# Loading k, v and q of the next batch but one at the end of slot 3, with q split first

## The chip, the cores and the metric

One NeuronCore of a Trainium2 chip runs the whole program; inputs and output lie in device memory. The metric is the device time of one execution in microseconds (us). The engines are PE (TensorE, matrix products; PEld is its weight load), DVE (VectorE), ACT (ScalarE), POOL (GpSimd) and SP (SyncE, which only issues DMAs here). Each works through its own instructions strictly in the order in which the program lists them; an instruction that waits holds up everything behind it on its engine.

## The reference

Three layers, one after the other. Shapes: 8 batches, 8 heads, 576 tokens, head width 64, 32 memory slots.

```
a    = softmax of phi over the tokens                        # per batch, head, slot
k_m  = a^T k ;  v_m = a^T v                                  # 32 x 64 per head
attn = softmax(q k_m^T / 8) ;  x = attn v_m                  # 4608 tokens x 512
g    = s * relu(x w_in)^2 + b ;  x2 = g w_out                # 512 -> 2048 -> 512
h    = x2 w_in2 ;  e = h * softmax(h) ;  out = layernorm(e) * g_ln @ w_out2
```

## The kernel before

Products that need more than half precision are made of three products of halves: an operand is split into a high and a low float16 part (`split_hi` on ACT, line 277; `split_lo` on DVE, line 280), after scaling by a power of two.

The order of the work is written out by hand. A long list of steps, `FIRST`, does batch 0, the decoding of the weights and part of batch 1. Then a loop over n = 1 to 7 does the feed-forward layer of batch n in two halves j (288 tokens each): `gemm1` (line 934) makes eight products of 12 matmuls into one of three PSUM buffers `hp`, and ACT takes each out with `relu` (line 945) and a square (line 970); DVE makes the two halves of the result (lines 920 and 977). Then four `gemm2` (line 994) follow, one for each d, each taken out by ACT (line 1011) and stored by SP (`gemm2_put`, line 1022). Before each `gemm2`, one of eight slots prepares the attention of batch n + 1:

- slots 0 and 1: the memory products `kv_mm`; the k and v of the batch are four pieces in three buffers, and piece 3 is loaded in slot 0. At the end of slot 1 the kernel before issues phi (line 295) and k, v pieces 0 to 2 (line 321) of batch n + 2. `q_abs` and `q_scale` find the scale of q.
- slot 2: `mem_scale`, `mem_hi`, `mem_lo` split the memory keys and values, and `mem_tr` (line 726) transposes them by DMA; then `q_split` of q pieces 0 and 1. A `q_split` is `q_hi` on ACT, `q_lo` on DVE, a transposing DMA `q_tr` (line 760) and, in the kernel before, the load of the same piece of batch n + 2 (line 331).
- slot 3: `q_split` of pieces 2 and 3, `phi_max`. The split goes to a work buffer with room for two pieces, so `q_hi` of piece 2 waits until `q_tr` of piece 0 has landed, and piece 3 waits for piece 1.
- slots 4 to 6: scores, softmax, and the transposing DMA `scores_T`; slots 4 to 7: `vw`, the memory values times w_in.

`gemm1` of the second half comes right after slot 3. Its first `relu` stands on ACT behind `q_hi` of pieces 2 and 3.

During n = 1 also w_in is split, in four pieces (`w_in_split`, before slots 0 to 5 in turn): ACT and DVE write a piece into `wt_s`, and SP moves it by four DMAs (`w_in_move`, line 606); the next piece waits for that move. In some slots `early` decodes a part of the third layer's weights: ACT's first step (line 228) waits for the DMA of line 1188, which the slot before issued on SP. In n = 5 such a decode stands in slot 3, in the other n not.

All DMAs of the loop are issued by SP, in program order.

Of the kernel before, what the change touches and what calls it, by code (L numbers as in the profile page):

```python
# [57 lines left out]
def tile_mem_attention__moe_relu2__solu_ln(  # L58
# [15 lines left out]
    nc = tc.nc  # L74
    NB, H, S, D = q.shape
# [4 lines left out]
    C = 6  # L80
# [4 lines left out]
    KD = DM // 128  # L85
# [57 lines left out]
    q_s = q_p.tile([128, 3, C, 2, D], FP32, name="q_s")  # L143
# [3 lines left out]
    def flat(t):  # L147
        n = len(t.shape)
        if n == 2:
            return t  # L150
        ax = " ".join("abcdef"[:n - 1])
        return t.rearrange(f"p {ax} -> p ({ax})")
# [120 lines left out]
    def absmax(out_, in_):  # L273
        nc.vector.tensor_reduce(out=out_, in_=in_, op=ALU.max, axis=AX, apply_absolute_value=True)  # L274

    def split_hi(hi, lo, src, sc):
        nc.scalar.activation(out=hi, in_=src, func=ACTF.Copy, scale=sc[:, 0:1])  # L277

    def split_lo(hi, lo, src, sc):
        nc.vector.scalar_tensor_tensor(  # L280
            out=lo, in0=src, scalar=sc[:, 0:1], in1=hi, op0=ALU.mult, op1=ALU.subtract
        )
# [6 lines left out]
    phi_t, kv_t, q_t = {}, {}, {}  # L289

    def load_phi(n):
        if n >= NB:
            return
        t = phi_p.tile([P, H, C, M], FP32, tag="phi", name="phi_sb")
        nc.sync.dma_start(
            out=t.rearrange("p h c m -> p h (c m)"), in_=phi[n].rearrange("h (p c) m -> p h (c m)", c=C)
        )
        phi_t[n] = t
# [8 lines left out]
    def q_place(n, i):  # L307
        if n and (n == 1 or i == 3):
            t = flat(wt_s)[:, i * C * 2 * D:]
        elif i == 3:  # L310
            t = flat(w_out_t[0]).bitcast(FP32)
        else:
            return q_s[:, i]
        return t[:, 0:C * 2 * D].rearrange("p (c h d) -> p c h d", c=C, h=2)

    def load_kv(n, i):
        if n >= NB:
            return
        t = kv_place(n, i)[0:P]
        for a, src in enumerate((k, v)):  # L320
            nc.sync.dma_start(
                out=t[:, a], in_=src[n, 2 * i:2 * i + 2].rearrange("h (p c) d -> p h (c d)", c=C)
            )
        kv_t[n, i] = t

    def load_q(n, i):
        if n >= NB:
            return
        t = q_place(n, i)[0:P]
        for a in range(2):  # L330
            nc.sync.dma_start(out=t[:, :, a, :], in_=q[n, 2 * i + a].rearrange("(p c) d -> p c d", c=C))  # L331
        q_t[n, i] = t


    es_t, km_t, qT_t, aT_t = {}, {}, {}, {}
# [4 lines left out]
    def phi_max(n):  # L340
        if n >= NB:
            return
        pm = e_p.tile([P, H, 1, M], FP32, tag="es", name="pm", bufs=1)
        phi_tree(n, pm[:, :, 0, :], ALU.max)
        if n < 2:
            px_t[n] = pm
            return
        px = e_p.tile([P, H, 1, M], FP32, tag="px", name="px", bufs=1)
        px_t[n] = pm, px

    def phi_tree(n, out_, op):
        ph = phi_t[n]
        t = e_p.tile([P, H, 2, M], FP32, tag="e", name="t")
        nc.vector.tensor_tensor(out=t, in0=ph[:, :, 0:2, :], in1=ph[:, :, 2:4, :], op=op)
        nc.vector.tensor_tensor(out=t, in0=t, in1=ph[:, :, 4:6, :], op=op)
        nc.vector.tensor_tensor(out=out_, in0=t[:, :, 0, :], in1=t[:, :, 1, :], op=op)
# [64 lines left out]
    def kv_mem(n, g):  # L421
        kv_mm(n, g)
        kv_sum(n, g)
        kv_out(n, g)
# [41 lines left out]
    def kv_out(n, g):  # L466
        kp = kp_t.pop((n, g))
        if g == 0:
            km_t[n] = e_p.tile([128, 2, 2 * D], FP32, tag="km", name="km", bufs=1)
        rs = st.tile([128, 1], FP32, tag="rs", name="rs")  # L470
        nc.vector.tensor_scalar(out=rs, in0=kp[:, 1, 0:1], scalar1=1e-9, scalar2=None, op0=ALU.add)
        nc.vector.reciprocal(out=rs, in_=rs)
        nc.vector.tensor_scalar(
            out=km_t[n][:, g], in0=kp[:, 0, 0:2 * D], scalar1=rs[:, 0:1], scalar2=None, op0=ALU.mult
        )
        if g == 0:
            if n > 1:
                load_kv(n, 3)
        else:
            phi_t.pop(n)  # L480
            es_t.pop(n, None)
            if n > 1:
                load_next_kv(n + 1)

    def load_next_kv(n):
        load_phi(n)
        for i in range(3):
            load_kv(n, i)

# [157 lines left out]
    def mem_all(n):  # L647
        al = st.tile([128, 2], FP32, tag="alb", name="al")
        nc.gpsimd.partition_all_reduce(out_ap=al, in_ap=bnd_t[n], channels=128, reduce_op=RED.max)
        bnd_t[n] = al  # L650
# [22 lines left out]
    def mem_scale(n):  # L673
        inv = st.tile([128, 2], FP32, tag="invb", name="inv")
        sc = pow2_scale(bnd_t.pop(n), inv, "scb", 2)
        sc_t[n] = c15
        cs = st.tile([128, KD], FP32, tag="cs", name="cs", bufs=2)
        t = st.tile([128, 1], FP32, tag="csa", name="csa", bufs=2)
        u = st.tile([128, 1], FP32, tag="csu", name="csu")
        nc.vector.tensor_tensor(out=u, in0=inv[:, 1:2], in1=iwin, op=ALU.mult)  # L680
        nc.vector.tensor_tensor(out=t, in0=s22, in1=u, op=ALU.mult)
        nc.vector.tensor_tensor(out=t, in0=t, in1=u, op=ALU.mult)
        csc_t[n] = cs, t
        msc_t[n] = sc
        es = st.tile([P, 1], FP32, tag="esc", name="esc", bufs=2)
        nc.vector.scalar_tensor_tensor(
            out=es, in0=inv[0:P, 0:1], scalar=scale, in1=qsc_t[n][1], op0=ALU.mult, op1=ALU.mult
        )
        esc_t[n] = es
# [3 lines left out]
    def work(i):  # L693
        if ("w", i) not in gt:
            gt["w", i] = raw_p.tile([128, 4096], FP16, tag="raw", name="work")
        return gt["w", i]
# [16 lines left out]
    def mem_hi(n):  # L713
        for ops in mem_ops(n):
            split_hi(*ops)

    def mem_lo(n):
        for ops in mem_ops(n):
            split_lo(*ops)
# [9 lines left out]
    qsc_t, esc_t = {}, {}  # L729

    def q_abs(n, i):
        if n not in qsc_t:
            qsc_t[n] = st.tile([P, KD], FP32, tag="qmx", name="qmx")
        absmax(qsc_t[n][:, i:i + 1], q_t[n, i].rearrange("p c h d -> p (c h d)"))

    def q_scale(n):
        mx = st.tile([P, 1], FP32, tag="qm", name="qm")
# [4 lines left out]
    def q_ops(n, i):  # L742
        u = slice((i % 2) * 1536, (i % 2 + 1) * 1536)
        qs = (work(0) if n > 1 else flat(kv_s[:, 2]).bitcast(FP16))[0:P, u]
        return qs, qs.rearrange("p (c h a d) -> p c h a d", c=C, h=2, a=2)

    def q_hi(n, i):
        qs = q_ops(n, i)[1]
        split_hi(qs[:, :, :, 0, :], None, q_t[n, i], qsc_t[n][0])

    def q_lo(n, i):
        qs = q_ops(n, i)[1]
        split_lo(qs[:, :, :, 0, :], qs[:, :, :, 1, :], q_t.pop((n, i)), qsc_t[n][0])

    def q_tr(n, i):
        if n > 1:
            qT = flat(qt_s).bitcast(FP16).rearrange("p (i x t) -> p i x t", i=KD, t=P)[:, i]
        else:
            qT = work(i // 2)[:, 0:24 * P].rearrange("p (i x t) -> p i x t", i=2, t=P)[:, i % 2]
        nc.sync.dma_start_transpose(out=qT, in_=q_ops(n, i)[0])  # L760
        qT_t[n, i] = qT.rearrange("p (c h) t -> p c h t", c=C)

    def q_split(n, i):
        q_hi(n, i)
        q_lo(n, i)
        q_tr(n, i)
        load_q(n + 1, i)

    def scores_mm2(n, cp):
        sp = ps_h.tile([128, 2, 512], FP32, tag="h", name="sp")  # L770
# [101 lines left out]
    def slot(n, i):  # L872
        if n >= NB:
            return
        if i == 0:
            kv_mem(n, 0)
            q_abs(n, 0)
            q_abs(n, 1)
        elif i == 1:
            kv_mem(n, 1)  # L880
            mem_bound(n)
            mem_all(n)
            q_abs(n, 2)
            q_abs(n, 3)
            q_scale(n)
        elif i == 2:
            mem_scale(n)
            mem_hi(n)
            mem_lo(n)
            mem_tr(n)  # L890
            q_split(n, 0)
            q_split(n, 1)
        elif i == 3:
            q_split(n, 2)
            q_split(n, 3)
            phi_max(n + 1)
            phi_all(n + 1)
        elif i == 4:
            scores_vw(n, 0)
        elif i == 5:  # L900
            scores_vw(n, 1)
        elif i == 6:
            scores_vw(n, 2)
        else:
            vw(n, 3)
            phi_sub(n + 1, nc.gpsimd)
            phi_exp(n + 1)
# [568 lines left out]
    with tc.manual_schedule():  # L1476
# [11 lines left out]
        for step in FIRST.split():  # L1488
            name, _, at = step.partition(".")
# [91 lines left out]
```

## Time and profile before

| | us |
|---|---|
| three runs, median (lowest, highest) | 1152.99 (1150.55, 1153.09) |
| the profiled execution, its time | 1154.11 |
| its span, first to last instruction | 1152.3 |
| PE busy | 1066.1 |
| DVE busy | 804.9 |
| ACT busy | 515.8 |
| POOL busy | 243.5 |

The `FIRST` list ends near 196 us, the loop over n runs to about 783 us, with about 81 us for one n, and then the third layer fills the rest, with PE busy nearly without a break. In the rows below, "us, us, engine line" of a timeline are the start, the duration, the engine and the line of the code; what stands in brackets is the engine's idle time before the instruction and who ended it.

### The profile page before, as it was taken

The numbers are of one execution on the slowest core, as the hardware profiler recorded it, in microseconds if no ns is written. First come the engines' busy times: TensorE is split into PE (matmuls) and PEld (weight loads), VectorE is DVE, ScalarE is ACT, GpSimd is POOL, SyncE is SP. The second block draws the span as 40 slices with busy tenths as digits, with TensorE's granted clock in tenths as the row PEclk, the third lists the DMA queues.
The fourth block names the chain that finished last, engine by engine and source line by source line (L and its number), as shares of the span: only waits on it lengthen the run. The fifth ranks groups of instructions, "written<-read, shape, count | busy, mean of one in ns | idle before, by whom it ended". The sixth has DMA issues, their size and how long they took to land.

```text
span 1152.3 us, 20462 instructions
## 1 busy us (share of the span) xinstructions
PE 1066.1 (93%) x8208; PEld 694.4 (60%) x8208; DVE 804.9 (70%) x1551; ACT 515.8 (45%) x745; POOL 243.5 (21%) x181
## 2 busy tenths in 40 slices
PE   0777699979999999999989999999999999999997
PEld 0644466756777777777767777765444444444443
DVE  5989968757776866876686786637666666666662
ACT  4365355444464455455355456623333333333332
POOL 2345721002103003012012010002222222222220
PEclk9778899989999999999999999999999999999999
DMA  9958143785392572662842414113445444455335
GB/s 289 264 142 206 39 81 88 174 151 125 100 189 65 131 145 70 161 115 65 197 104 67 122 32 164 58 44 84 102 104 110 101 107 93 103 110 101 81 67 101
DMA packets 246368, 134.00 MB, mean 116 GB/s; under 512 B 177152, under 2 KB 234496, under 8 KB 246272
## 3 DMA queue, kind: packets, MB, share of 16 engines
q1 hardware_dynamic: 246176, 132.68, 50.1%
q8 instruction: 64, 1.05, 0.4%
q14 instruction: 32, 0.26, 0.1%
q0 software_dynamic: 96, 0.01, 0.0%
HBM read 71.83 MB, written 23.07 MB: 82 GB/s over the span
## 4 chain that ended last, share of the span: by engine, by line
PE 66%; DVE 5%; DMA 3%; ACT 2%; SPq 2%; issue 1%; POOL 1%; POOLq 0%; ACTq 0%; DVEq 0%
PE y L994 21%; PE hp L1327 16%; PE y L1409 15%; PE hp L934 10%; PE wp L626 1%; PE kp L432 1%; DMA work<-in_moe_w_out_dram 1%; DMA qt_s<-work 1%; DVE g L977 1%; PE sp L773 1%; SPq L760 1%; DMA kv_s<-in_v_dram 1%; SPq L331 0%; DVE wt_s L280 0%; DMA w_in_t<-wt_s 0%
## 5 line engine op out<-in xcount | busy, mean ns | idle before, releaser
L994 PE MATMUL y<-g,w_out 128*128 128x288 f16 (+1 forms) x2880 | 366.2, 288 | 7.4 <-DVE first L180 6.9
L994 PEld LDWEIGHTS <-w_out 128*128 128x128 f16 x3072 | 297.9, 98 | 100.6 <-issue 20.4
L934 PE MATMUL hp<-aT,vwt 128*128 128x288 f16 x1536 | 199.4, 291 | 17.4 <-ACT r L945 14.1
L1409 PE MATMUL y<-w_t,lt 128*128 128x512 f16 x864 | 192.0, 379 | 1.8 <-DMA lt<-nat 1.8
L1327 PE MATMUL hp<-w_t,xs 128*128 128x512 f16 x864 | 192.2, 379 | 0.0
L934 PEld LDWEIGHTS <-vwt 128*128 128x128 f16 x1536 | 151.8, 99 | 62.0 <-issue 20.5
L1409 PEld LDWEIGHTS <-lt 128*128 128x128 f16 x864 | 84.4, 98 | 103.8 <-DMA lt<-nat 2.3
L1327 PEld LDWEIGHTS <-xs 128*128 128x128 f16 x864 | 84.5, 98 | 101.5
L1371 POOL TENSOR_TENSOR rstd<-ve,nhalf 128x1 f32<-128x1 f32 x36 | 52.7, 1463 | 336.1 <-DVE mv L1369 336.1
L1341 DVE TENSOR_REDUCE hmx<-hp 128x1 f32<-128x1024 f32 x36 | 44.1, 1224 | 86.7 <-PE hp L1327 86.7
L277 ACT ACTIVATE xs<-xt,xsc 128x512 f16<-128x512 f32 x36 | 26.0, 721 | 151.3 <-PE hp L1327 129.9
L977 DVE TENSOR_TENSOR g<-r,g 128x576 f16<-128x576 f32 x115 | 89.8, 780 | 5.5 <-POOL r L972 1.6
L970 ACT ACTIVATE r<-r 128x576 f32<-128x576 f32 x118 | 80.6, 683 | 22.4 <-DVE g L977 18.2
L1011 ACT ACTIVATE x<-y,bcol,cs 128x288 f32<-128x288 f32 x64 | 37.4, 584 | 113.6 <-PE y L994 84.3
L945 ACT ACTIVATE r<-hp 128x576 f32<-128x576 f32 x120 | 76.7, 640 | 10.7 <-PE hp L934 6.7
L1348 ACT ACTIVATE e<-hp,nm,xiv 128x1024 f32<-128x1024 f32 x36 | 43.3, 1202 | 46.2 <-DVE nm L1343 46.2
L274 DVE TENSOR_REDUCE xmx<-x 128x1 f32<-128x288 f32 x64 | 28.6, 447 | 46.0 <-ACT x L1011 46.0
L920 DVE CAST g<-r 128x576 f16<-128x576 f32 x112 | 51.3, 458 | 10.9 <-ACT r L970 10.8
L849 POOL TENSOR_TENSOR e<-e,ssm 96x512 f32<-96x512 f32 x21 | 21.9, 1045 | 171.1 <-DVE ssm L844 169.0
L1417 ACT ACTIVATE o<-y,io 128x512 f32<-128x512 f32 x36 | 24.7, 687 | 51.7 <-issue 43.2
L1385 DVE TENSOR_TENSOR nat<-so,nat 128x1024 f16<-128x1024 f32 x36 | 43.8, 1216 | 5.4 <-ACT nat L1380 5.4
L1364 DVE BATCH_NORM_STATS2 bs<-so 128x6 f32<-128x512 f32 x72 | 46.3, 685 | 1.3
(239 smaller groups left out, 1213.0 us busy)
## 6 DMA issues: line engine op xcount, KB each, us to landing
x_d<-x SPq DMA_DIRECT2D x64, 144.0 KB, 2.8
xt<-x_d SPq DMA_DIRECT2D x36, 256.0 KB, 3.2
kv_s<-in_k_dram SPq DMA_DIRECT2D x31, 288.0 KB, 7.3
kv_s<-in_v_dram SPq DMA_DIRECT2D x31, 288.0 KB, 7.5
q_s<-in_q_dram SPq DMA_DIRECT2D x42, 144.0 KB, 4.0
phi_sb<-in_phi_dram SPq DMA_DIRECT2D x8, 576.0 KB, 6.2
out_dram<-o SPq DMA_DIRECT2D x24, 192.0 KB, 2.4
raw<-in_moe_w_out_dram SPq DMA_DIRECT2D x4, 1024.0 KB, 7.8
```

The costliest lines, as they stand in the source:

```text
L920: nc.vector.tensor_copy(out=g_of(n, j, 0)[:, 2 * fp:2 * fp + 2, 0:BLK], in_=gt["r2", j, fp])
L934: nc.tensor.matmul(out=hp[:, u, 0:BLK], lhsT=vt[:, pw, R, f * 128:(f + 1) * 128], rhs=aT[:, CJ * j:CJ * (j + 1), pa, R, :], start=(x == 0) ...
L945: nc.scalar.activation(out=r, in_=gt.pop(("h", j, fp))[:, :, 0:BLK], func=ACTF.Relu, scale=scale)
L970: nc.scalar.activation(out=r2, in_=r, func=ACTF.Square)
L977: (nc.vector if eng == "D" else nc.gpsimd).tensor_tensor(out=g_of(n, j, 1)[:, fs, 0:BLK], in0=gt.pop(("r2", j, fp)), in1=g_of(n, j, 0)[:, ...
L994: nc.tensor.matmul(out=y[:, 0:w], lhsT=w_out_t[d][:, pw, f, :], rhs=g_of(n, j, pg)[:, f, 0:w], start=(x == 0), stop=(x == len(steps) - 1),)
L1327: nc.tensor.matmul(out=hp[:, a, :], lhsT=xs[:, px, kk, :], rhs=wt[:, pw, kk, a * 512:(a + 1) * 512], start=(kk == 0 and px == 0 and pw == ...
L1341: nc.vector.tensor_reduce(out=mx, in_=hv, op=ALU.max, axis=AX)
L1364: nc.vector.bn_stats(out=bs[:, a, :], in_=so[:, a * 512:(a + 1) * 512])
L1371: nc.gpsimd.tensor_tensor(out=rstd, in0=ve, in1=nhalf, op=ALU.pow)
L1385: nc.vector.tensor_tensor(out=nat[:, 1, :], in0=so, in1=nat[:, 0, :], op=ALU.subtract)
L1409: nc.tensor.matmul(out=y[:, 0:DM], lhsT=lt[:, pl, f, :], rhs=wt[:, pw, f, :], start=(x == 0), stop=(x == len(steps) - 1),)
```

## The change

Three things. q_s keeps the two heads of a piece one after the other instead of interleaved, for all batches but the first, so that one partition of one head is one run of 6 x 64 numbers in memory; the transposed q is indexed to match. The load of q moves out of `q_split`, and the load of k, v pieces 0 to 2 out of slot 1; both stand in one function `load_next` that slot 3 calls after its `q_split`s: eight q DMAs, then six for k and v. phi keeps its place. And slot 2 does `q_split` 0 and 1 ahead of the memory's scale, split and transpose.

```
@@ q_place
-            return q_s[:, i]
-        return t[:, 0:C * 2 * D].rearrange("p (c h d) -> p c h d", c=C, h=2)
+            t = flat(q_s[:, i])
+        t = t[:, 0:C * 2 * D]
+        if n:
+            return t.rearrange("p (h x) -> p h x", h=2)
+        return t.rearrange("p (c h d) -> p c h d", c=C, h=2)
@@ load_q
         for a in range(2):
-            nc.sync.dma_start(out=t[:, :, a, :], in_=q[n, 2 * i + a].rearrange("(p c) d -> p c d", c=C))
+            if n:
+                nc.sync.dma_start(out=t[:, a], in_=q[n, 2 * i + a].rearrange("(p c) d -> p (c d)", c=C))
+            else:
+                nc.sync.dma_start(out=t[:, :, a, :], in_=q[n, 2 * i + a].rearrange("(p c) d -> p c d", c=C))
@@ kv_out
             if n > 1:
-                load_next_kv(n + 1)
-
-    def load_next_kv(n):
-        load_phi(n)
+                load_phi(n + 1)
+
+    def load_next(n):
+        for i in range(KD):
+            load_q(n, i)
         for i in range(3):
             load_kv(n, i)
@@ q_abs, q_ops, q_hi, q_lo
...
-        return qs, qs.rearrange("p (c h a d) -> p c h a d", c=C, h=2, a=2)
+        return qs, qs.rearrange("p (x a d) -> p x a d", a=2, d=D), flat(q_t[n, i]).rearrange("p (x d) -> p x d", d=D)
...
@@ q_tr
-        qT_t[n, i] = qT.rearrange("p (c h) t -> p c h t", c=C)
+        qT_t[n, i] = qT.rearrange("p (h c) t -> p c h t", c=C)
@@ q_split
         q_tr(n, i)
-        load_q(n + 1, i)
@@ slot
         elif i == 2:
+            q_split(n, 0)
+            q_split(n, 1)
             mem_scale(n)
             mem_hi(n)
             mem_lo(n)
             mem_tr(n)
-            q_split(n, 0)
-            q_split(n, 1)
         elif i == 3:
             q_split(n, 2)
             q_split(n, 3)
+            load_next(n + 1)
             phi_max(n + 1)
             phi_all(n + 1)
```

## Rows read from the trace of the kernel before

**Rows 1.** The page: busy time, share of the span and instructions of each engine.
```profile
PE 1066.1 (93%) x8208; PEld 694.4 (60%) x8208; DVE 804.9 (70%) x1551; ACT 515.8 (45%) x745; POOL 243.5 (21%) x181
```

**Rows 2.** Waits of PE: who ended them, us in total, times, longest.
```profile
PE hp L934 <- ACT r L945: 14.1, 7, 7.9
```

**Rows 3.** Windows, n = 1 and n = 2: length, busy times, PEclk, DMA share, GB/s.
```profile
196.00:291.00 95.00, 84.93 (x785) 64.10 (x784) 65.62 (x119) 47.28 (x67) 11.95 (x10) 0.93 0.71 150
291.00:372.30 81.30, 81.11 (x791) 62.53 (x789) 59.05 (x118) 42.43 (x66) 13.90 (x11) 1.00 0.58 123
```

**Rows 4.** Windows around three gaps of PE, columns as in rows 3.
```profile
238.80:246.65 7.85, 0.00 (x0) 0.00 (x0) 2.04 (x3) 2.90 (x5) 0.00 (x0) 0.71 0.89 196
246.65:252.35 5.70, 5.70 (x24) 3.60 (x24) 5.53 (x10) 4.33 (x7) 1.50 (x1) 0.50 0.78 145
...
276.30:279.60 3.30, 3.30 (x19) 2.03 (x16) 2.44 (x5) 1.72 (x2) 0.83 (x1) 0.50 1.03 225
...
578.40:581.70 3.30, 0.00 (x1) 0.00 (x0) 1.25 (x4) 1.69 (x4) 1.09 (x1) 1.00 1.24 252
```

**Rows 5.** Timeline of n = 1, slots 2 and 3.
```profile
224.43 0.57 ACT L1011 ACTIVATE x<-y,bcol,cs 128x288 f32<-128x288 f32 x1
...
226.94 3.40 SPq L606 DMA_DIRECT2D w_in_t<-wt_s  x4
...
231.75 3.80 SPq L726 DMA_TRANSPOSE work<-work  x1
...
235.65 3.51 SPq L760 DMA_TRANSPOSE qt_s<-work  x1
...
241.26 0.93 ACT L277 ACTIVATE work<-q_s,sc 96x768 f16<-96x768 f32 x1 [10.07 <-issue]
242.23 1.01 DVE L280 SCALAR_TENSOR_TENSOR work<-q_s,sc,work 96x768 f16<-96x768 f32 x1 [10.00 <-ACT work L277]
...
244.66 0.93 ACT L277 ACTIVATE work<-wt_s,sc 96x768 f16<-96x768 f32 x1 [2.46 <-DMA qt_s<-work]
...
246.65 10.28 PE L934 MATMUL hp<-aT,vwt 128*128 128x288 f16 x60 [7.86 <-ACT r L945]
```

**Rows 6.** Timeline of n = 5, slots 2 and 3.
```profile
562.81 0.45 DVE L274 TENSOR_REDUCE xmx<-x 128x1 f32<-128x288 f32 x1 [0.15 <-ACT x L1011]
...
564.38 1.13 DVE L280 SCALAR_TENSOR_TENSOR work<-km,sc,work 128x128 f16<-128x128 f32 x4
...
574.60 0.43 SPq L1188 DMA_DIRECT2D work<-in_moe_w_out_dram  x1
...
579.98 0.66 ACT L228 ACTIVATE work<-work 128x512 f32<-128x512 f32 x1 [4.15 <-DMA work<-in_moe_w_out_dram]
...
581.71 7.57 PE L934 MATMUL hp<-aT,vwt 128*128 128x288 f16 x60 [3.31 <-ACT r L945]
```

**Rows 7.** Timelines of n = 6, slots 2 and 3, SP and ACT.
```profile
652.65 3.10 SPq L760 DMA_TRANSPOSE qt_s<-work  x2
...
656.29 0.93 ACT L277 ACTIVATE work<-q_s,sc 96x768 f16<-96x768 f32 x1 [1.90 <-DMA qt_s<-work]
657.87 0.94 ACT L277 ACTIVATE work<-wt_s,sc 96x768 f16<-96x768 f32 x1 [0.64 <-DMA qt_s<-work]
```

**Rows 8.** Timeline, last k, v load of n = 3; then DMA queues of 398:403 (packets, MB, share).
```profile
396.57 1.41 SPq L321 DMA_DIRECT2D kv_s<-in_v_dram  x1
...
q1 hardware_dynamic: 885, 1.23, 111.0%
```

**Rows 9.** Timeline of n = 1, slots 4 and 5: third and fourth piece of w_in.
```profile
262.64 3.67 SPq L606 DMA_DIRECT2D w_in_t<-wt_s  x4
...
270.24 2.00 ACT L277 ACTIVATE wt_s<-w_in_t,wsc 128x2048 f16<-128x2048 f32 x1 [0.73 <-DMA w_in_t<-wt_s]
```

**Rows 10.** Timeline of the FIRST list, q of batch 1; then DMA queues of 130:134.
```profile
153.99 0.95 DVE L274 TENSOR_REDUCE qmx<-wt_s 96x1 f32<-96x768 f32 x1 [0.75 <-DMA wt_s<-in_q_dram]
...
q1 hardware_dynamic: 1184, 0.30, 32.6%
```

More of the change, by code (lines that the diff above doesn't have):

```diff
@@ L733, in q_abs @@
             qsc_t[n] = st.tile([P, KD], FP32, tag="qmx", name="qmx")
-        absmax(qsc_t[n][:, i:i + 1], q_t[n, i].rearrange("p c h d -> p (c h d)"))
+        absmax(qsc_t[n][:, i:i + 1], flat(q_t[n, i]))
     def q_scale(n):
@@ L744, in q_ops @@
         qs = (work(0) if n > 1 else flat(kv_s[:, 2]).bitcast(FP16))[0:P, u]
-        return qs, qs.rearrange("p (c h a d) -> p c h a d", c=C, h=2, a=2)
+        return qs, qs.rearrange("p (x a d) -> p x a d", a=2, d=D), flat(q_t[n, i]).rearrange("p (x d) -> p x d", d=D)
     def q_hi(n, i):
-        qs = q_ops(n, i)[1]
-        split_hi(qs[:, :, :, 0, :], None, q_t[n, i], qsc_t[n][0])
+        _, qs, src = q_ops(n, i)
+        split_hi(qs[:, :, 0], None, src, qsc_t[n][0])
     def q_lo(n, i):
-        qs = q_ops(n, i)[1]
-        split_lo(qs[:, :, :, 0, :], qs[:, :, :, 1, :], q_t.pop((n, i)), qsc_t[n][0])
+        _, qs, src = q_ops(n, i)
+        split_lo(qs[:, :, 0], qs[:, :, 1], src, qsc_t[n][0])
     def q_tr(n, i):
```

## The prediction

> **What bounds the kernel now.** I read the busy shares first: PE is busy for 1066.1 of 1152.3 us [rows 1], so the program can shorten only where PE stands idle or runs slowly. Next, who ends PE's waits: in the loop over batches the largest is gemm1's wait for a `relu` on ACT, 14.1 us in seven pieces, one of 7.9 [rows 2]. Then windows of one n each: n = 2 takes 81.30 us with PE busy throughout, n = 1 takes 95.00 at a mean clock of 0.93 [rows 3]. Nearly all that the loop can give back lies in n = 1, and a little in n = 5. Fine windows show what it is [rows 4]. From 238.80 to 246.65 PE does nothing; in that gap the granted clock falls to 0.50, that is from 2.4 to 1.2 GHz, and PE works at it for 5.70 us more, which costs half of that, 2.85. In n = 5 there is a gap of 3.30 at full clock. The timeline says why. In n = 1 `q_hi` of pieces 2 and 3 starts only at 241.26 and 244.66, because the transposes of pieces 0 and 1 have not landed, and the first `relu` of the half stands behind them on ACT [rows 5]. The SP rows ahead show the source: `mem_tr` occupies SP for 3.80 us and the first `q_tr` for 3.51, behind the k, v loads of slot 1 and a move of w_in. With nothing being loaded, in n = 6, two `q_tr` together occupy SP for 3.10, and `q_hi` of piece 2 starts 3.64 after the first is issued, piece 3 at 1.58 after that [rows 7]; PE has no gap there. In n = 5 a decode also stands in front of the `relu`, waiting for a load that SP issued only at 574.60, behind two pairs of q loads [rows 6].
>
> **The change, part by part, in n = 1.** *Split first.* ACT is free after 224.43 + 0.57 = 225.0. Two `q_hi` of 0.93 end at 226.9; DVE finishes its piece of w_in at 226.94 (when SP starts moving it), then a short maximum, then two `q_lo` of 1.01, at 228.3 and 229.3. SP moves w_in until 230.34 and stores one x, 0.6: the first `q_tr` can be issued at 231.0 instead of 235.65 [rows 5]. Its landing: 3.64 after the issue by the quiet case of rows 7, 5.61 by n = 1 itself (235.65 to 241.26). With the k, v loads gone only the move of w_in is ahead, so I take 4.5, nearer to the quiet case: `q_hi` of piece 2 at 235.5, piece 3 at 1.6 after that, 237.1, done at 238.0, one x of 0.57 and a `relu` of about the same: 239.3. PE has filled its three buffers at 238.80, so a gap of 0.5 is left, by the late landing 2.5; I take 1.0. Gain: 7.85 - 1.0 = 6.9. The clock stayed at full through the 3.30 us of n = 5 [rows 4], so a gap of 1.0 should not lower it: another 2.85. What is pushed back is the memory's scale and split (2.25 on DVE, from the end of the x maximum at 563.26 to 565.51 in n = 5 [rows 6]) and `mem_tr`, now behind both `q_tr`. Their result is first read by the scores in slot 4, a whole gemm1 later (96 matmuls, 12.1 us at the 60 in 7.57 of rows 6); that gemm1 is the cover, and if it were gone the price would be a transpose's issue and landing, 1.55 + 3.64 by rows 7. On ACT the next x of gemm2 stands behind them; its PSUM buffer is wanted again only after gemm1.
>
> *The loads in slot 3.* Eight q DMAs and six of k, v, all on SP behind the last `q_tr`. They wait for nothing new: every buffer was last read by a `kv_mm` or `q_lo` that is over. SP pays 0.43 for an issue that nothing hinders [rows 6] and 1.41 for one behind a full queue [rows 8]: 14 of them are 6.0 to 19.7 us. The data, 8 x 144 + 6 x 288 = 2880 KB = 2.95 MB, takes 12.0 us at the 1.23 MB that 5 us of k, v loads moved [rows 8]. Behind them on SP stands the store of x of d = 3; the x tiles have three buffers, so ACT needs that one back only three gemm2 later. The first things that anyone waits for come in slot 4, behind that gemm1: the `scores_T`, and in n = 1 the move of w_in's third piece. That piece's writing is tied to the end of gemm1 and so comes 9.8 earlier, at 262.64 - 9.8 = 252.8; the last `q_tr` is issued at 239.1, when its `q_lo` ends, and takes 1.5, so the data of the loads runs from about 241 until 253. The move meets its tail: 0.8 us later, between 0 and the rival's price below, and since the fourth piece already waits for that move [rows 9], I count the 0.8 in full. The loaded data is used from the next n on, behind four gemm2.
>
> *In n = 5.* SP loses four q issues and does `q_tr` earlier; I work the load of the decode out at 570.4 instead of 574.60, from the start of slot 2 (about 562.8: the second `q_hi` ends at 564.7, the second `q_lo` at 565.8, two `q_tr` of 1.55 by 567.9, the memory's split 2.25 after `q_lo`, at 568.0, `mem_tr` 1.55, a store and the load 0.43 each) [rows 6, 7]. Landing 5.38 later as before [rows 6] is 575.8; decode, x and `relu` end at 577.7, ahead of the 578.40 where PE runs out. The gap of 3.3 goes, less 0.3 for a margin that is only 0.7. The others of the seven waits, 2.9 in sum, I leave as they are.
>
> *Longer runs in memory.* The same bytes, a sixth of the packets. In the FIRST list DVE waits 0.75 for the last q of batch 1 [rows 10], a wait that shorter issues can cut; most of it then meets the next wait for PE: 0.3, between 0 and 0.75. The trace gives a price for the packets: two q loads of 256-byte packets used 32.6% of 4 us for 0.30 MB, which is 70 engine-us per MB over 16 engines [rows 10]; k, v loads with 1536-byte packets used 111.0% of 5 us for 1.23 MB, 72 per MB [rows 8]. So the size of the packet buys no transfer time here. The Trainium skill, "DMA: Bandwidth & Descriptors", section Specifications, says otherwise: under 512 bytes the engine reads, modifies and writes, and full rate is not reached. By that rule the q loads of batch 1 would land sooner and the whole wait of 0.75 would go, 0.45 more than I count; this trace does not show the penalty, and I go by the trace.
>
> **Sum.** -6.9 - 2.85 - 3.0 - 0.3 + 0.8 = -12.3. From the profiled execution's 1154.11 that is 1141.8; this execution lies 1.1 above the median of the runs shown, so I forecast 1140.7.
>
> **Rivals.** (a) *Half of it:* the move of w_in, not the k, v loads, is what holds the transposes in n = 1. For it: it is issued at 226.94, right ahead of them [rows 5]. Then only the 2.25 of the reorder and some 1.5 of queue are won: a gap near 4 and a clock that falls as before: 3.8 + 3.0 - 0.8 = 6.0, at 1147.0. Against it: the move occupies SP for 3.40 and is over before 231.
>
> (b) *Hidden anyway:* ACT's late `q_hi` is set by the transposes' own time, and the 10.07 that the row gives to "issue" [rows 5] is not a wait for data. Then the gap stays, n = 5 gains a microsecond or two: 1151.5. Against it: rows 7, where the same transposes without loads leave PE no gap.
>
> (c) *Slower:* the loads, 14 in one burst, stand ahead of w_in's third piece on SP. The fourth waits for it on ACT, and behind it all of slot 5. If SP pays 1.41 an issue it is free only at 240.6 + 19.7 = 260.3, 7.5 late; if the four moves are then held like the 3.80 of `mem_tr` instead of 0.9 each, 11.6 more. PE's gap there grows by 19.1 and the clock falls for as long as after 246.65: 1140.7 - 0.8 + 19.1 + 2.9 = 1161.9. It decides from a landing about 10 us late (12.3 + 0.8 less the 2.9). For it: rows 5 show SP held just so behind six k, v loads and a move, and 9 shows that nothing is spare. Against it: the loads begin 12 us ahead of the move and their data takes 12.0. The Trainium skill, "DMA: Bandwidth & Descriptors", section Queues, rings and completion order, has SP on one row of rings whose descriptors are consumed in order: by that rule the move lands behind the whole burst, as this rival needs, and the 3.80 and 3.51 of rows 5 agree with it.
>
> **How the numbers follow.** Within 0.3% (3.5 us) of the median is no change that can be told. Forecast 0.66, its own range 1136 to 1145 (gap left 0 to 2.5; clock falling in it or not, 2.85; n = 5 0 to 3.3; the second fall of the clock, 276.30 to 279.60 [rows 4], going too, 1.65). (a) 0.18, (b) 0.09, (c) 0.07, of which 0.01 is no change. So faster 0.84, same 0.10, slower 0.06. The range runs from 1134 to 1148.5: it takes in (a) and leaves out (b), (c) and a little below.
>
> **What would show it.** Right: the gap at 238.80 at most 2.5 us and no stretch at half clock near it; `mem_tr` and `q_tr` on SP near 1.6 each; in n = 5 no gap in the second gemm1; n = 1 near 86 us, the others as they are. Wrong: w_in's third move landing more than 8.5 us after it is issued and a larger gap in slots 5 and 6 of n = 1 (c); `q_hi` of piece 2 still over 5 us behind its transpose (a); the gap of 7.85 unchanged though SP is quiet (b).

## Result, and the profile after

The changed kernel takes 1138.81 us (median of 4 runs, 1138.68 to 1140.08) against 1153.04 (1150.55 to 1154.46) for the kernel before in the same comparison: ratio 0.9883 [0.9868, 0.9899], 14.2 us faster. Forecast was 1140.7, within a range of 1134.0 to 1148.5. The profiled execution took 1138.68 with a span of 1136.9; against before's profiled execution it is 15.4 shorter, and the sums below are made between these two.

Busy times on the page after; they answer to [rows 1]:

```profile
PE 1060.9 (93%) x8208; PEld 691.5 (61%) x8208; DVE 804.7 (71%) x1551; ACT 517.8 (46%) x745; POOL 242.2 (21%) x181
```

PE has as many matmuls, and is busy 5.2 us less: part of the gain is clock, the rest idle time. PE's waits in the kernel after (who ended them, us in total, times, longest), beside [rows 2]:

```profile
PE hp L942 <- ACT r L953: 4.1, 6, 2.3
PE wp L634 <- DVE e L797: 3.4, 1, 3.4
```

gemm1's wait for a `relu` fell from 14.1 us to 4.1. The second row is the weight product of slot 6 in n = 1, and its wait was 2.2 before (the recorded expectations place this gap in slot 5). Windows after, columns as in rows 3: n = 1, n = 2, what is left of the gap of [rows 4], and the stretch behind slot 6's gap:

```profile
193.45:279.77 86.32, 82.08 (x786) 62.57 (x784) 65.49 (x119) 46.92 (x67) 11.65 (x10) 0.98 0.72 164
279.77:361.40 81.63, 81.27 (x790) 62.57 (x789) 59.34 (x118) 42.77 (x66) 13.23 (x11) 1.00 0.55 123
236.28:236.72 0.44, 0.00 (x1) 0.00 (x0) 0.44 (x2) 0.41 (x2) 0.00 (x0) 1.00 0.35 66
264.40:267.20 2.80, 2.80 (x21) 1.11 (x21) 1.98 (x3) 1.42 (x2) 0.00 (x0) 0.50 0.75 160
```

n = 1 went from 95.00 [rows 3] to 86.32, n = 2 stayed. The gap of 7.85 is 0.44, with one of 0.38 five us later, and the first half clock of [rows 4] is gone; the second is still there. The timeline of n = 1 after, slots 2 to 6, answers to [rows 5] and [rows 9]:

```profile
228.76 3.61 SPq L768 DMA_TRANSPOSE qt_s<-work  x2
...
232.46 1.56 SPq L734 DMA_TRANSPOSE work<-work  x1
233.33 0.94 ACT L277 ACTIVATE work<-q_s,sc 96x768 f16<-96x768 f32 x1 [4.62 <-issue]
...
234.72 0.94 ACT L277 ACTIVATE work<-wt_s,sc 96x768 f16<-96x768 f32 x1 [0.46 <-DMA qt_s<-work]
...
235.34 2.96 SPq L768 DMA_TRANSPOSE qt_s<-work  x2
...
236.72 4.57 PE L942 MATMUL hp<-aT,vwt 128*128 128x288 f16 x36 [0.44 <-ACT r L953]
...
238.36 3.59 SPq L335 DMA_DIRECT2D q_s<-in_q_dram  x6
...
244.61 0.87 PE L780 MATMUL sp<-work,qt_s 128*96 128x64 f16 x16
...
245.38 0.52 SPq L324 DMA_DIRECT2D kv_s<-in_v_dram  x1
...
247.26 1.99 ACT L277 ACTIVATE wt_s<-w_in_t,wsc 128x2048 f16<-128x2048 f32 x1
...
251.66 3.51 SPq L614 DMA_DIRECT2D w_in_t<-wt_s  x4
...
259.32 2.00 ACT L277 ACTIVATE wt_s<-w_in_t,wsc 128x2048 f16<-128x2048 f32 x1 [0.79 <-DMA w_in_t<-wt_s]
...
264.36 1.90 PE L634 MATMUL wp<-w_in_t,work 128*32 128x512 f16 x16 [3.42 <-DVE e L797]
```

Transposes now hold SP for 1.48 to 1.81 each, not 3.80 and 3.51. `q_hi` of piece 2 starts 4.57 after the first `q_tr` is issued, and piece 3 at 1.39 after that. The 14 loads occupy SP from 238.36 to 245.90, under gemm1. The last rows are the path through w_in, whose third piece is split right before slot 4 and whose fourth right before slot 5: the third split starts 2.65 after slot 4's scores at 244.61 (before, 1.47: 256.77 and 258.24); the fourth, which waits for the third's move, starts 7.66 after that move's issue (7.60 before [rows 9]); and the gap in slot 6 is 3.42.

How far the same matmul has moved ahead of its place before, with what each stretch adds:

```
n=1, first gemm1             195.21 -> 192.68    -2.53
n=1, slot 2's gemm1          234.22 -> 231.71    -2.51   (+0.02)
n=1, scores of slot 4        256.77 -> 244.61   -12.16   (-9.65)
n=2, first gemm1             290.84 -> 279.61   -11.23   (+0.93)
n=5, first gemm1             534.81 -> 523.06   -11.75   (-0.52)
n=5, scores of slot 4        589.12 -> 573.84   -15.27   (-3.52)
from 793 us to the end                          -15.40   (-0.13)
```

In n = 5 [rows 6] the decode's load goes out on SP 3.34 before the second gemm1 starts; before, it went out 0.77 after that start, at 573.83. PE runs through:

```profile
558.74 0.43 SPq L1196 DMA_DIRECT2D work<-in_moe_w_out_dram  x1
...
562.08 11.19 PE L942 MATMUL hp<-aT,vwt 128*128 128x288 f16 x90
563.86 0.67 ACT L228 ACTIVATE work<-work 128x512 f32<-128x512 f32 x1 [3.95 <-DMA work<-in_moe_w_out_dram]
```

In the FIRST list DVE waited for batch 1's q twice: 1.35 for the third piece and 0.75 for the last [rows 10]. Before, from the maximum of the second piece to q's scale (`qm`), which reads all four:

```profile
148.42 0.94 DVE L274 TENSOR_REDUCE qmx<-wt_s 96x1 f32<-96x768 f32 x1
...
151.10 0.95 DVE L274 TENSOR_REDUCE qmx<-wt_s 96x1 f32<-96x768 f32 x1 [1.35 <-DMA wt_s<-in_q_dram]
...
155.83 0.14 DVE L738 TENSOR_REDUCE qm<-qmx 96x1 f32<-96x4 f32 x1
```

After, the third piece's wait is 0.21 and the last one's is gone:

```profile
147.84 0.94 DVE L274 TENSOR_REDUCE qmx<-wt_s 96x1 f32<-96x768 f32 x1
...
149.37 0.95 DVE L274 TENSOR_REDUCE qmx<-wt_s 96x1 f32<-96x768 f32 x1 [0.21 <-DMA wt_s<-in_q_dram]
...
153.42 0.14 DVE L746 TENSOR_REDUCE qm<-qmx 96x1 f32<-96x4 f32 x1
```

### The profile page after: what moved, and what is told of

The parts are those of the page before. It is cut to its first block, busy times and chain, and to the rows that moved or that the text cites. A ratio compares the mean times of both kernels' runs of the same rounds, so it can differ in the third digit from the quotient of the medians.

```text
span 1136.9 us, 20489 instructions
## 1 busy us (share of the span) xinstructions
PE 1060.9 (93%) x8208; PEld 691.5 (61%) x8208; DVE 804.7 (71%) x1551; ACT 517.8 (46%) x745; POOL 242.2 (21%) x181
## 4 chain that ended last, share of the span: by engine, by line
PE 69%; DVE 4%; DMA 3%; ACT 2%; SPq 1%; issue 1%; POOL 0%; POOLq 0%; ACTq 0%
PE y L1002 24%; PE hp L1335 16%; PE y L1417 15%; PE hp L942 10%; PE wp L634 2%; PE kp L438 1%; DMA work<-in_moe_w_out_dram 1%; PE sp L780 1%; DVE g L985 1%; DVE wt_s L280 0%; DMA w_in_t<-wt_s 0%; DMA kv_s<-in_k_dram 0%; DMA lt<-nat 0%; SPq L335 0%; DMA qt_s<-work 0%
```

## Experiments

The theory: the loads between slot 1 and slot 3 held the transposes on SP, and with that `q_hi`, the `relu` behind it and PE; the order of slot 2 and the layout add little. The rivals: the move of w_in alone holds them; or the order does most; or the burst costs something in slots 4 to 6. Each edit is shown against the changed kernel. Figures for one stretch (FIRST, slots of n = 1, n = 5) are shifts of the profiled execution against that of the kernel before, as in the list above. Each kernel has one profile; that of e3 lies 1.9 below the median of its runs, that of e7 2.9 above. In the four kernels in which FIRST is the same (before, e2, e3, e6) the first gemm1 of n = 1 starts at 193.44 to 195.21, so a shift of FIRST below 1.8 says little.

**Each part alone.** `e1_layout` has only the new layout:

```
 slot 1:  load_phi(n + 1)
+         load_kv(n + 1, 0..2)         # as before
 load_next:  load_q, load_kv  ->  return
 q_split: + load_q(n + 1, i)           # as before
 slot 2:  mem_scale, mem_hi, mem_lo, mem_tr ahead of q_split 0, 1
```

> Only the layout of q is changed; loads and order of slot 2 as in the kernel before. My theory (the wait of q_hi for its transpose in slots 2 and 3 is the loss, and the size of the packets buys only shorter issues): FIRST list 0.5 to 2.5 us shorter, the gap of n = 1 (7.86) shorter by at most 2, n = 5's gap (3.31) by at most 1; total 2 to 5 us less than before. Rival (256-byte packets of the q loads are what holds the transposes up): the gap of n = 1 falls under 4 and half clock near it is gone, total 8 or more less.

Measured 1150.55, ratio 0.9983 [0.9972, 0.9994]: 2.4 us. n = 1 keeps its gap (7.26) and its half clock; the gain is 1.80 in FIRST, about what its two shorter waits on q give, and 0.88 in n = 1. The layout alone doesn't touch the stall, but isn't nothing either.

`e2_loads` has only the moved loads:

```
 q_place, load_q: if n:  ->  if False:     # 256-byte packets
 q_tr:   "p (h c) t"  ->  "p (c h) t"
 slot 2: mem_scale, mem_hi, mem_lo, mem_tr ahead of q_split 0, 1
```

> Only the loads of q and of k, v 0 to 2 are moved to the end of slot 3; old layout, memory split first. Theory: most of the gain is here: gap of n = 1 at 2 to 4 us, no half clock next to it or a short one, gap of n = 5 gone, FIRST list unchanged: 8 to 11 us less than before. Rival (the order of slot 2 is what counts): gap of n = 1 still over 5 with half clock behind it, total under 5 less.

Measured 1143.83, 0.9928 [0.9913, 0.9943]: 9.1 us. The gap in n = 1 is 1.45, less than the 2 to 4 expected, without a fall of the clock, and n = 5 gains 3.21: the loads are the main cause, and rival (a), by which the move of w_in does the holding, falls. But slots 4 to 7 give back 2.78. The timeline shows why:

```profile
240.95 4.64 SPq L337 DMA_DIRECT2D q_s<-in_q_dram  x6
...
254.29 3.81 SPq L614 DMA_DIRECT2D w_in_t<-wt_s  x4
...
263.36 2.00 ACT L277 ACTIVATE wt_s<-w_in_t,wsc 128x2048 f16<-128x2048 f32 x1 [2.19 <-DMA w_in_t<-wt_s]
...
268.40 1.90 PE L634 MATMUL wp<-w_in_t,work 128*32 128x512 f16 x16 [4.84 <-DVE e L797]
```

w_in's third move lands 9.07 after issue, not 7.60, and slot 6's gap is 4.84. A move that lands late behind the burst is rival (c)'s mechanism, at a small part of its price.

`e3_order` has only slot 2's new order:

```
 q_place, load_q, q_tr, slot 1, load_next, q_split: all as before
 slot 2: q_split 0, 1 ahead of mem_scale, mem_hi, mem_lo, mem_tr
```

> Only slot 2's order is changed: q split 0 and 1 ahead of the memory; loads in their old places, old layout. Theory: the first transpose is issued about 4 us earlier in n = 1 but behind the k, v loads and the move of w_in, and the second still behind a pair of q loads: gap of n = 1 at 4 to 6, clock still falls, n = 5's gap 1 to 3: 3 to 6 us less than before. Rival (order is what counts): gap under 2, total 9 or more less.

Measured 1150.00, 0.9973 [0.9961, 0.9985]: 2.9 us, just under the 3 to 6 expected. The first transpose, now in front, is what gets held:

```profile
230.41 4.23 SPq L767 DMA_TRANSPOSE qt_s<-work  x1
...
238.84 0.94 ACT L277 ACTIVATE work<-q_s,sc 96x768 f16<-96x768 f32 x1 [8.46 <-issue]
```

`q_hi` comes 8.43 after it and a gap of 5.41 is left, with the clock falling for 6.8 us.

**Two parts of three.** `e5_no_order` is the changed kernel with slot 2's order as before; `e6_no_layout` has 256-byte packets for q; `e7_no_loads` has the loads in their old places:

```
e5: slot 2: mem_scale .. mem_tr ahead of q_split 0, 1
e6: q_place, load_q: if n: -> if False:;  q_tr: "p (c h) t"
e7: slot 1: load_kv(n + 1, 0..2);  q_split: load_q(n + 1, i);  load_next: return
```

> The whole change but for slot 2's order (memory first, then q split 0 and 1). Theory: with the loads gone from slots 1 and 2 the order is worth only mem_tr's 1.5 us on SP and the wait for the memory's scale: gap of n = 1 1.5 to 3 where the whole change has 0.44, nothing else; 1 to 3 us above the whole change. Rival (order and move are each needed): gap over 4 and half clock back, 6 or more above.

> The whole change but for q's layout. Theory as it stands after the first runs: FIRST list 0.9 to 1.7 us longer than with the layout; the burst of slot 3 takes longer on SP and in the queue, so the move of w_in's third piece lands later and the gap in slot 5 of n = 1 is 4.5 to 5.5 instead of 3.42, with a longer stretch of half clock: in sum 3 to 4 us above the whole change. Rival (packet size matters for the FIRST list alone): gap in slot 5 stays at 3.4, 1 to 2 us above.

> New layout and new order, loads in their old places. Theory: the k, v loads and the q issues still stand around the transposes: gap of n = 1 at 3 to 5, n = 5's gap 0.5 to 1.5, FIRST list 2 us shorter: 5 to 8 us less than the kernel before. Rival (layout and order suffice): gap of n = 1 under 1.5, within 2 us of the whole change.

Measured: e5 1141.75, 0.9904 [0.989, 0.9918]; e6 1141.16, 0.9902 [0.9887, 0.9918]; e7 1146.13, 0.9939 [0.9925, 0.9953]. So taking one part out of the whole costs 2.9 (order), 2.4 (layout, where 3 to 4 was expected) and 7.3 (loads). That the single parts sum to 2.4 + 9.1 + 2.9 = 14.4 and measure 14.2 together is chance, for stretch by stretch they are not additive. In slots 2 and 3 of n = 1 they gain 0.88 + 8.64 + 2.60 = 12.12 alone and 9.65 together, in n = 5 0.41 + 3.21 + 1.44 = 5.06 alone and 3.52 together: there they shorten the same wait. In slots 4 to 7 of n = 1 they give back 2.67 alone and 0.93 together. e7's gap in n = 5 is 2.41, with 3.4 us at half clock, where 0.5 to 1.5 was expected: order and layout alone do not clear it. In e6 the gap in n = 1 is 0.36, as good as with the layout, but slots 4 to 7 give back 3.19: what the layout buys in the loop it buys there.

**Which loads.** `e10_kv_only` is the changed kernel with the loads of q left in `q_split`, so only k and v moved:

```
 load_next: only load_kv(n, 0..2)
 q_split: + load_q(n + 1, i)
```

> The whole change, but the q loads stay in q_split (k, v loads at the end of slot 3). Theory by parts: in n = 1 k, v loads were the larger hindrance (1.77 MB in front of the transposes), so the gap of n = 1 is 1 to 3; in n = 5 the q issues in front of the decode's load leave a gap of 0 to 2: 1 to 4 us more than the whole change. Rival (the q issues between the transposes are the hindrance): gap of n = 1 over 4, 6 or more above the whole change.

Measured 1143.12, 0.9914 [0.9899, 0.9929]: 3.0 faster than e7 and 4.3 slower than the whole, a little over the 1 to 4 expected. The k, v loads decide in n = 1 (slots 2 and 3: 3.12 in e7, 8.15 here, 9.65 whole), the q loads in n = 5 (here 0.26 lost, whole 3.52 gained). n = 5 with q's loads between the transposes:

```profile
563.33 0.57 SPq L1195 DMA_DIRECT2D work<-in_moe_w_out_dram  x1
...
568.94 0.66 ACT L228 ACTIVATE work<-work 128x512 f32<-128x512 f32 x1 [5.97 <-DMA work<-in_moe_w_out_dram]
...
570.67 9.18 PE L941 MATMUL hp<-aT,vwt 128*128 128x288 f16 x60 [1.96 <-ACT r L952]
```

The decode's load goes out 0.81 before gemm1, not 3.34, and a gap of 1.96 stays, behind which the clock falls for 3.4 us.

**What gives back time in slots 4 to 7.** `e14_no_burst` leaves out slot 3's loads of q and of k, v pieces 0 to 2 for batches 3 to 7; those batches work on data already there:

```
 load_kv: for a, src in enumerate((k, v) if n < 3 or i == 3 else ()):
 load_q:  for a in range(2 if n < 3 else 0):
```

> The whole change without the loads of slot 3: q and k, v pieces 0 to 2 of batches 3 to 7 are not loaded, old data is used in their place. Theory: the loads cost nothing where they stand, save up to 0.8 us in n = 1: the third piece's move lands 7.4 to 7.7 us after its issue (7.66 with the loads), gap in slot 5 2.5 to 3.5, total 0 to 1.5 us under the whole change. Rival (the burst is what makes that gap 3.42): gap under 1.5 and no half clock there, 3 or more under the whole change.

Measured 1139.05, 0.9874 [0.986, 0.9889]: not told apart from the whole change. The third move without a burst ahead of it:

```profile
252.58 3.42 SPq L614 DMA_DIRECT2D w_in_t<-wt_s  x4
...
259.87 2.00 ACT L277 ACTIVATE wt_s<-w_in_t,wsc 128x2048 f16<-128x2048 f32 x1 [0.41 <-DMA w_in_t<-wt_s]
...
264.91 1.90 PE L634 MATMUL wp<-w_in_t,work 128*32 128x512 f16 x16 [3.06 <-DVE e L797]
```

It lands after 7.29 instead of 7.66: in these two traces the burst costs 0.4 us of gap. A gap of 3.06 remains with none of slot 3's loads, so they are not what made it grow from 2.21. The clock falls for 6.8 us here and for 3.4 in the whole change, so slots 4 to 7 give back 1.88, more than with the burst.

`e11_layout1` is the changed kernel with the new layout for batch 1's q alone; the bursts have 256-byte packets:

```
 q_place, load_q: if n:  ->  if n == 1:
 q_tr: "p (h c) t" if n == 1 else "p (c h) t"
```

> The whole change, with the new layout for batch 1's q alone (loaded in the FIRST list); the q of the later batches is loaded in 256-byte runs as in the kernel before. Theory: the FIRST list is as short as in the whole change (first gemm1 of n = 1 1.5 to 2.5 us earlier than in the kernel before), and the gap in slot 5 of n = 1 is about 5 us as without the layout: 1 to 2.5 us above the whole change. Rival (the FIRST list varies by itself and the layout has no part in it): first gemm1 at less than 1 us earlier.

Measured 1140.52, 0.9891 [0.9876, 0.9905]. Slots 4 to 7 give back 3.79, the move lands after 9.07, the gap is 4.83. Against the whole change that is 1.7 us of median, with intervals that overlap; in the profile slots 4 to 7 give back 2.86 more, 1.41 of it gap and the rest slower matmuls, at half clock for 6.8 us instead of 3.4. The three kernels with 256-byte packets in the burst (e2, e6, e11) agree in this: the layout's worth in the loop lies in the bursts of the later batches.

Eleven traces together give the gap in slot 6 as a sum of four pieces: from slot 4's scores to the start of the third split (the lag); 4.40 from there to the issue of its move; from that issue to the start of the fourth split, which waits for the move (the landing); and 5.04 from the fourth split to PE's product. From the sum goes 16.33, in which PE has other work:

```
kernel         lag    landing   sum     gap seen   clock in gemm1
before         1.47    7.60     2.18    2.21       falls
e7_no_loads    1.47    7.29     1.87    1.93       falls
e3_order       1.47    7.56     2.14    2.18       falls
e1_layout      1.47    7.58     2.16    2.20       falls
e10_kv_only    2.65    7.46     3.22    3.23       full
e14_no_burst   2.65    7.29     3.05    3.06       full
whole change   2.65    7.66     3.42    3.42       full
e5_no_order    2.65    7.91     3.67    3.68       full
e2_loads       2.64    9.07     4.82    4.84       full
e11_layout1    2.65    9.07     4.83    4.83       full
e6_no_layout   2.65    9.38     5.14    5.14       full
```

The constants are from the whole change; the other lines are not fitted. The lag is 1.47 wherever the clock falls in gemm1 and 2.65 wherever it doesn't: at full clock PE gets ahead of ACT's chain by 1.18 us more, and the chain through w_in hands that back as a gap. That each row sums to the gap seen shows the path. That the lag follows the clock is a pattern over eleven traces and not shown: no run changed the clock by itself, and where it falls the gap in front of gemm1's last five products is also longer (4.58 to 7.86 against 0.36 to 1.94). The landing is late where the burst ahead has 256-byte packets.

**Moving that chain.** `e8_piece3_late` is the changed kernel with w_in's fourth piece split before slot 6 instead of slot 5:

```
-if n == 1 and j == 1 and d < 2:        w_in_split(d + 2)
+if n == 1 and j == 1 and d in (0, 2):  w_in_split(2 + d // 2)
```

> The whole change, and in n = 1 the split of w_in's fourth piece stands before slot 6 instead of slot 5, so that ACT does not wait for the third piece's move there. Theory: the gap of 3.42 in slot 5 and the half clock behind it go (4.3 us with the slower matmuls), while slot 7's product with that piece waits 0 to 2 us for its move: 2 to 4 us less than the whole change. Rival (the gap moves to slot 7): same time as the whole change within 1 us, a gap of 3 or more in front of slot 7's matmuls.

Measured 1148.20, 0.9958 [0.9946, 0.9971]: a miss, 9.4 slower than the whole change, where 2 to 4 less was expected. The wait moves to slot 7, and the clock falls for 13.7 us around it:

```profile
267.43 1.99 ACT L277 ACTIVATE wt_s<-w_in_t,wsc 128x2048 f16<-128x2048 f32 x1
...
271.83 3.75 SPq L614 DMA_DIRECT2D w_in_t<-wt_s  x4
...
279.15 0.59 PE L634 MATMUL wp<-w_in_t,work 128*32 128x512 f16 x1 [10.23 <-DMA w_in_t<-wt_s]
```

PE itself needs the piece, 7.3 after its issue; there was no slack to push it into.

`e12_piece2_slot3` goes the other way: the third piece is split in slot 3 ahead of the loads, the fourth before slot 4. `e13_piece2_slot2` does so at the end of slot 2:

```
+slot 3 (e12) or slot 2 (e13):  if n == 2: w_in_split(2)
-if n == 1 and j == 1 and d < 2:   w_in_split(d + 2)
+if n == 1 and j == 1 and d == 0:  w_in_split(3)
```

> The whole change, and in n = 1 the third piece of w_in is split in slot 3, behind q's splits and ahead of the loads, the fourth before slot 4. Theory (the gap of 3.42 in slot 5 is the fourth piece waiting on ACT for the third one's move): that gap and its half clock go, 4.3 us, and 2 to 3.5 come back in front of gemm1's relu, which now waits for 2.0 us more of ACT: 0.5 to 2.5 us less than the whole change. Rival (the piece's place does not matter, the chain of ACT and DVE is what is full): within 0.5 us of the whole change or above it.

> The same with the third piece at the end of slot 2, ahead of q's splits 2 and 3, where ACT waits 4.6 us for the first transpose anyway. Theory: gemm1's gap 1 to 1.5 (0.44 in the whole change), the scores of slot 4 wait 1 to 3 us because the last transposes are issued later, no gap in slot 5: 0.5 to 3 us less than the whole change. Rival (the second piece's move has not landed, so ACT stands and q's splits come late): gap at gemm1 over 4, above the whole change.

Measured e12 1140.29, 0.9887 [0.9872, 0.9901]; e13 1138.45, 0.9875 [0.9859, 0.9892]: neither is told apart from the whole change, and the gain expected (0.5 to 2.5 us, 0.5 to 3 us) is not seen. In e13 slot 6's gap is 0.53 and slots 4 to 7 gain 3.04 on before, but `relu` is late again, in n = 1 and by 1.43 in the first gemm1 of n = 2:

```profile
236.50 4.57 PE L944 MATMUL hp<-aT,vwt 128*128 128x288 f16 x36 [0.52 <-ACT r L955]
...
242.87 3.10 PE L944 MATMUL hp<-aT,vwt 128*128 128x288 f16 x24 [1.80 <-ACT r L955]
```

The split is the same 2.0 us of ACT wherever it stands, so the wait changes its place. No version that beats the change was found.

## Why the prediction was right

*The gap and the clock in n = 1.* Forecast 6.9 + 2.85 = 9.75, measured 9.65 in slots 2 and 3: PE's idle time there went from 7.86 to 0.82, and the rest of the stretch from 14.69 to 12.08, 2.61 for the clock. The steps hold one by one. n = 1 starts 2.53 earlier; with that taken off, the forecast had the first `q_tr` at 228.5 (measured 228.76), `q_hi` of piece 2 at 233.0 (233.33) and of piece 3 at 234.6 (234.72), the first `relu` done at 236.8 (236.67), and a gap of 0.5, for which 1.0 was entered (0.44). The value chosen for the landing, 4.5 between 3.64 and 5.61, was 4.57. The reorder's cover held: the scores of slot 4 start right behind gemm1.

*Which part does it.* The forecast put it on the k, v loads and, against rival (a), not on the move of w_in. e2 (loads alone, gap 1.45) and e1 (loads in place, 7.26) show that it is the loads, e10 against e7 (8.15 against 3.12 in slots 2 and 3) that it is mostly those of k, v. Rival (b) is refuted too: `q_hi` did wait for what SP held.

*n = 5.* Forecast 3.0, measured 3.52, of which 3.31 is the gap. The decode's load was put at 570.4, which is 558.7 after the shift of 11.75 so far; it went out at 558.74 and its row starts 5.12 later (5.38 forecast). e10 shows that it is the q loads, as the step said: with them in place the gap stays at 1.96.

*FIRST.* Forecast 0.3 within 0 and 0.75; measured 2.5 (2.08 from 149 to 195 us, 0.45 ahead of it): the mis-sized term. I counted one wait on batch 1's q, of 0.75, missed the one of 1.35 ahead of it, and took most of the gain to meet the next wait for PE. From the second of the four maxima to q's scale the list now takes 5.59 instead of 7.41. In the ten traces of kernels with the new layout for batch 1 this stretch takes 5.58 to 6.12, in the four without it 6.94 to 7.50, so some 1.5 us of it belong to the layout. No other wait took the gain back: from q's scale to the first gemm1 of n = 1 it is 39.26 us, and was 39.38. The other 0.7 of the 2.5 is no larger than the spread of FIRST between kernels in which it is the same, and is not put down to the change.

*The burst in front of w_in's third move.* Forecast +0.8, measured +0.93 in slots 4 to 7, but the reason given was wrong, and that the sizes agree is luck. The move's landing was nearly as before (7.66 to 7.60), because SP was through with its issues 5.8 us ahead of it. What came late was the split in front of the move: the forecast moved it up with the end of gemm1, by the same lag as before, and the lag is 1.18 longer. e14 shows that the burst is not the cause: without it the gap is still 3.06. With that gap the second half clock stayed as well, which the forecast's own range had allowed to go.

*"The size of the packet buys no transfer time."* This step failed. My two prices, 70 and 72, came from stretches under different load [rows 8, 10], one light and one full: they could not show it. The fair comparison for the light one is the same two loads of q in the kernel after, in 1536-byte packets (DMA queues of 129.4:133.4):

```profile
q1 hardware_dynamic: 224, 0.30, 26.4%
```

That is 56 engine-us per MB against 70. From the packets of these two loads it comes to 54 to 59 in the ten traces with the new layout for batch 1 and to 71 or 72 in the four without. Where the loads are dense the size shows too: with 256-byte packets in the burst the third move lands after 9.07 to 9.38 rather than 7.66 (e2, e6, e11). Two windows inside the bursts, q in 256-byte packets in e2:

```profile
244.00:248.00 4.00, 3.69 (x40) 3.12 (x39) 3.87 (x8) 3.91 (x7) 0.00 (x0) 1.00 1.02 214
```

and mostly k, v, in 1536-byte packets, in the kernel after:

```profile
246.00:250.00 4.00, 4.00 (x41) 2.83 (x30) 3.30 (x6) 3.69 (x5) 0.00 (x0) 1.00 1.06 262
```

Per MB that is 16 x 1.02 / 0.214 = 76 engine-us against 16 x 1.06 / 0.262 = 65, and SP issues six q loads in 4.64 instead of 3.59. The Trainium skill, "DMA: Bandwidth & Descriptors", section Specifications, has packets under 512 bytes short of the full rate; the rows agree in the direction, with a quarter more engine time per MB under light load and a sixth more in the burst. The prediction set that rule aside in favour of its two prices; the wait of 0.75 that would go by the rule did go.

*Rival (c).* Its mechanism exists: with 256-byte packets ahead the move lands more than 8.5 after issue, the mark set for it. It costs 1.4 to 1.7 us of gap, 1.9 to 2.9 in slots 4 to 7 with the longer half clock, and not 19: behind the first load of the burst SP paid 0.42 to 0.63 for one of q and for most of k, v near 0.45, not 1.41, and its issues ended before the move was due. The 3.80 and 3.51 of rows 5, which the prediction counts for (c), are times for which SP was held; the landing, which (c) is about, is 7.66 behind the burst and 7.29 without it.

*The sum.* 9.65 + 3.52 + 2.53 - 0.93 and 0.6 elsewhere make 15.4 between the profiled executions; the medians differ by 14.2, the forecast by 12.3. The terms in the loop came out within 0.6 each; most of what is left is FIRST.

## What to carry to other kernels

Before pricing a moved load, look at what its queue does in between: a transfer that nobody is waiting for can hold a short transpose behind it that everybody waits for, and the place for a burst is behind the last such step, with enough time before the next. Price the same step by a stretch of the trace in which the queue is quiet; that gave the whole timeline here to 0.4 us. Compare the prices of two kinds of packet only under the same load: taken from a light and a full stretch, 70 and 72 hid a difference of a quarter. And when PE is made faster ahead of a chain that runs at ACT's pace, look for part of the gain to come back as a wait at that chain's end: here 1.2 us.

## What was not expected of the hardware

The clock's fall does not follow the length of the gap beside it. At full clock throughout were gaps of 3.30 (before, n = 5 [rows 4]), 2.89 (e1, n = 5) and 2.36 (e12, n = 1). A fall of 3.4 us came with gaps of 1.96 (e10, n = 5), 2.21 (before, slot 6) and 3.42 (after, slot 6), and one of 6.8 with 3.06 (e14, slot 6). The 5.70 us at 1.2 GHz in n = 1 before had cost 2.61; by that rate 3.4 us cost some 1.6, an estimate. So a change that only shortens a gap may keep the fall, and the price of a fall is to be taken with a chance, not as certain.
